# Three pairs without slot sums where score tiles change tokens, slots without a row spread over the rest, row buffers lent later once

## The chip, the cores and the metric

The kernel runs on one core of a Trainium2 chip. The metric is the device time of one execution in microseconds (us); the median of several executions counts. TensorE is called PE in the profile (its weight loads PEld), VectorE is DVE, ScalarE is ACT, GpSimd is POOL, and SyncE (SP) issues most transfers.

## The reference

The input is 2048 tokens of width 512. A layer norm `xn` feeds two branches, and the result is `x + A(xn) + B(xn)`.

```python
# A: attention, 32 heads of width 16 that share one k and one v
q = (xn @ wq).reshape(B, S, H, Dh).transpose(0, 2, 1, 3)
scores = jnp.einsum("bhqd,bkd->bhqk", q, xn @ wk) * (Dh ** -0.5)
A = heads_joined(softmax(scores) @ (xn @ wv)) @ wo
# B: product-key experts, H = 32, E = 64 keys on each side, K = 2
q = jnp.einsum("nd,dhc->nhc", xf, w_q)          # 2 halves of 128
s1, s2 = q1 @ k1.T, q2 @ k2.T                   # 64 scores each
i1, i2 = top 2 of each;  cand = the 4 sums;  top_e = the best 2 of 4 (rows of u and v)
g = softmax(top_s)
act = gelu(einsum("nd,nhkd->nhk", xf, u[top_e]))
out = einsum("nhk,nhk,nhkd->nd", g, act, v[top_e])
```

So each token takes 64 expert rows of 4096: a dot with `u`, a gelu and a gate, and a weighted sum of `v`.

## The kernel before

**Pairs.** After a start phase the kernel runs a list of 256 steps, `d` = 0 to 255. Each step is a *pair*: attention over two blocks of 128 keys for one unit (512 queries, 4 heads; 16 blocks make a unit, 32 units in all). `att_steps` emits for a pair, in this order: four score matmul groups (`sc`, L326) whose exponentials ScalarE writes to `pt` (L329), the `pv` matmuls of the pair before (L340), then `mid()`, four more score groups, perhaps an output projection (`block_out`, `pwo`), and `fill()`. All engines take their instructions in the order in which this list emits them.

**The expert branch** lies beside attention in the same pairs. Tokens are split into four groups of 512. For groups 0 and 1 the experts are *gathered*: 512 slots, each one row of `u` and `v` for 128 tokens. `gather` (L970, POOL) brings 128 rows of 4 KB into a row buffer `g`; `dot` (L982, DVE) multiplies with the token; ScalarE's tanh makes the gelu; `add` (L1017, DVE) adds the weighted `v` row to the token's total. This last is a *slot sum*. For groups 2 and 3 the experts are computed *densely* (`dense`: one-hot gates, then 32 blocks of `pact`, L727, and `pout`, L855). Before either, the scores of all four groups are computed by `item`: one item is 128 tokens by 8 score halves, 12 matmuls `psc` (L531) in four parts of three, then 8 MAX8 (L544) and 8 FIND_INDEX8 (L546) on VectorE. PSUM has three `x` buffers for this.

**Who sets the order.** `score_thread` is a generator of items and dense blocks; `fill()` advances it by parts until a planned amount (`aim`, at most `MOST`) is reached. The order of groups and weight chunks is `SEQ`: group 0 (8 chunks), group 1 (2 chunks), group 2 (8, then its dense part), group 1 (6 more), group 3 (8, then its dense part). Where the group changes, the four `xt` tiles (512 KB each) of the new tokens replace the old ones: `load_phase2_xt` (L1086, on SP's queue) issues each as soon as the last item of the old group has used its predecessor. SP also issues the reads of score weights (`wp_read`, L504: `wk<-dw`).

**The slots' pace.** `mid()` emits `todo` dots, a weight step, and `sums` slot sums; each slot sum sets one row buffer free, and `gathers(4)` then issues as many gathers as buffers are free, at most four:

```python
todo = max(min(int(pos + 0.001), g_next[0]) - d_next[0], 0)
sums = min(a_ready[0] - a_next[0], max(todo, 3) if d < half else 4)
if dense_on[0] > 2: sums = min(sums, 2)
if quiet[0] > 0: quiet[0] -= 1; sums = 0
while g_next[0] < NSL and g_next[0] < a_next[0] + NGB - lent[0] and most > 0: gather(...)
```

`pos` grows per pair by a rate that depends on the stage: 2.1 while group 0 is scored, 1.75 later (2.3 for 12 pairs after a dense part), 2.6 in a dense part, and in the last quarter what is left over what remains of the list. `g_next`, `d_next` and `a_next` count gathers, dots and sums; `a_ready` is the number of slots whose tanh has been issued (in fours). There are `NGB` = 12 row buffers; `lent` = 2 holds two of them back for the output weights `wo`, from the pair that sets it until the last of four `block_out`s. `quiet` exists already: in each dense part it stops the sums for three pairs at the end of the one-hot stage.

The gather of a token tile's first slot also loads that tile's `xa` (totals and normed tokens) through SP's queue.

Of the kernel before, what the change touches and what calls it, by code (L numbers as in the profile page):

```python
# [34 lines left out]
TPH = GT  # L35
NPH = NGRP
NSP = 2
NB = 32
# [17 lines left out]
def tile_kernel(ctx, tc, x, wq, wkv, wo, wqT, kT, uv, ub, vb, out):  # L56
# [416 lines left out]
    def wk_tile():  # L473
        return big.tile([P, 2, 512], F32R, name="wk", tag="wk", bufs=NWK)
# [26 lines left out]
    def wp_read(n, ks=range(KC)):  # L501
        for k in ks:
            wk = wk_tile()
            nc.sync.dma_start(raw(wk[:]), d_w[SEQ[n][1]][:, k])  # L504
            WC.setdefault(n, []).append(wk)
# [6 lines left out]
    def item(n_, ti, make=()):  # L512
        ph, c = SEQ[n_]
        nph, nc_ = SEQ[n_ + 1] if n_ + 1 < len(SEQ) else (None, None)
        t = TPH * ph + ti
        g, j = divmod(t, GT)
        b, jb = divmod(ti, BT)
        if jb == 0:
            m8 = small.tile([P, BT, 8, 8], F32, name="m8", bufs=1)
            i8 = small.tile([P, BT, 8, 8], U32, name="i8", bufs=1)  # L520
            M8[ph, c, b], I8[ph, c, b] = m8, i8
        m8, i8 = M8[ph, c, b], I8[ph, c, b]
        p = xtile("psc")

        last = ti == TPH - 1
        more = nc_ is not None and not (ph >= NSP and c == NC - 1)
        read = more and n_ + 1 >= NC
        n = 0
        for k in range(KC):
            for a, bb in TERMS:  # L530
                nc.tensor.matmul(p, XT[g][k][:, a, j * P:(j + 1) * P], WC[n_][k][:, bb, :],  # L531
                                 start=n == 0, stop=n == 11)
                n += 1
            if read and ti == 0 and k < 2:
                wp_read(n_ + 1, range(2 * k, 2 * k + 2))
            if last and more and nph != ph:
                load_phase2_xt(nph, k)
            if k < KC - 1:
                yield 3 * UNIT
            if k == 1:  # L540

                yield from islice(make, 1)
        for s in range(8):
            nc.vector.max(m8[:, jb, s, :], p[:, s * E:(s + 1) * E])  # L544
        for s in range(8):
            nc.vector.max_index(i8[:, jb, s, :], m8[:, jb, s, :], p[:, s * E:(s + 1) * E])  # L546
        if jb == BT - 1:
            batch(ph, c, b)
        yield 3 * UNIT
# [100 lines left out]
    def dense(DG, after):  # L650
# [211 lines left out]
        for b in range(NB):  # L862
            wd = []
            if b > 1:
                if b not in halved:

                    yield None
                if b not in halved:
                    flush()
                p = xtile("pact")  # L870
                for k in activations(b, splits[b][0], p):
                    if k == 0:
                        store(lambda b=b: fetch_gates(b + 1))
                        if b % 2 == 0 and b > 2:
                            later_split(b + 2)
                        if b == 2:

                            store(load_totals)
                    if k == KC - 1 and b == NB - 1 and after is not None:
                        wp_read(after, range(2))  # L880
                    if b == NB - 1 and after is not None:
                        load_phase2_xt(SEQ[after][0], k)
                    if k < KC - 1:
                        yield 3 * UNIT

                if b not in fetched:
                    if b > 3 and formed[0] < b - 2:
                        flush()
                    run(STORES)
                    assert b in fetched  # L890
            vs = splits.pop(b)[1]
            gy = gates[b]
            if b > 2:
                gates.pop(b - 1)
            g, y = (gy[:, 0, :], gy[:, 1, :]) if b > 1 else (gy[:, b, :], hh[:, b, :])

            def gated(g=g, p=None):
                stt(g, g, 1.0 / GS, p, op0=OP.mult, op1=OP.mult)

            def whole(y=y, g=g):  # L900
                stt(y, y, 1.0, g, op0=OP.add, op1=OP.mult)

            def scaled(y=y, g=g):
                multiplied[0] += 1
                stt(g, g, 1.0 / GS, y, op0=OP.mult, op1=OP.mult)

            def high(y=y if b > 1 else g, wd=wd):
                wd.append(late[0].tile([P, 2, 512], F32R, name="wd", tag="wd", bufs=4))
                nc.scalar.copy(wd[0][:, 0, :], y)
                behind(lambda: low(y, wd[0]))  # L910

            def low(y, wd):
                nc.vector.tensor_tensor(out=wd[:, 1, :], in0=y, in1=wd[:, 0, :], op=OP.subtract)  # L913
                formed[0] += 1

            if b > 1:
                nc.scalar.activation(y, p, AF.Square, scale=C_CUB ** 0.5)
                stt(y, y, C_IN, p, op0=OP.add, op1=OP.mult)
                LAST.append(lambda y=y: nc.scalar.activation(y, y, AF.Tanh))
                if b == 3:  # L920

                    behind(lambda gated=gated, g=g, p=p: gated(g, p))
                else:
                    gated(g, p)
                behind(whole)
                LATER_ACT.append(high)
            else:
                LATER.append(lambda scaled=scaled, high=high: (behind(scaled), on_act(high)))
            held.append((wd, vs))
            if b > 1:  # L930
                yield 3 * UNIT
            if b == 3:
                later_split(4)
            if b == 4:
                dense_on[0] = 1
            for _ in range(b - 1 if b in (2, 3) else 0):
                if out_ready():
                    block_out()
                    yield 3.6
            if b % 2:  # L940
                if b > 1:
                    later_split(b + 2)
                if ready:
                    for _ in range(2):
                        if formed[0] < used[0] + 2:
                            yield None
                    yield from sums()
                ready, held = held, []
# [73 lines left out]
    g_next, d_next, a_next, a_ready = [0], [0], [0], [0]  # L1022
# [90 lines left out]
    dense_on, quiet = [0], [0]  # L1113
# [19 lines left out]
    STEPS = 512  # L1133


    def att_steps(d, mid, fill):
        i = 2 * d
# [40 lines left out]
        if i == STEPS + 2:  # L1178
            last_out_a(3)
            last_out_b()  # L1180
        if i >= 124 and i % 128 == 124 or i == STEPS - 30:
            lent[0] = 2
        if 128 <= i < STEPS and i % 128 == (26 if i // 128 == 2 else 10) or i == STEPS - 10:
            load_wo()
# [57 lines left out]
    with tc.manual_schedule(engines={E_.PE, E_.Activation, E_.DVE, E_.Pool, E_.SP}):  # L1242
        done0 = spent[0]
        half = STEPS // 2
        pos, since = 0.0, half
        for d in range(half + 24):
# [6 lines left out]
            else:  # L1253
                pos += (2.1 if len(IDX) < NC * TPH else 2.3 if 0 <= d - since < 12 else 1.75, 0, 1.4, 1.5, 0.5)[dense_on[0]]

            todo = max(min(int(pos + 0.001), g_next[0]) - d_next[0], 0)

            def mid():
# [107 lines left out]
```

## Time and profile before

| what | value |
|---|---|
| median of 3 runs | 1934.66 us (1933.02 to 1942.46) |
| the profiled execution, its own time | 1943.82 us |
| its span, first to last instruction | 1942.1 us |
| mean granted PE clock | 0.978 |
| PE, DVE, ACT, POOL busy | 1870.5, 1675.0, 1294.5, 562.6 us |
| bytes moved by DMA | 491.11 MB, 253 GB/s over the span |

The start phase takes the first 138.6 us; then come the 256 pairs. A pair with 15 `psc`, `pact` or `pout` matmuls beside attention takes 6.81 us, one with 18 takes 7.49 us. A pair's start is taken as the start of its first exponential (every fourth `pt` row of L329). So pair 31 starts at 370.1 us, 34 at 389.3, 38 at 419.3, 41 at 443.3, 64 at 605.5, 65 at 618.9, 131 at 1065.6, 135 at 1093.2, 136 at 1102.9, 143 at 1151.2, 156 at 1241.3, 159 at 1260.4, 184 at 1442.0, 209 at 1597.1, 253 at 1905.1. Rows of a window give the time in which each engine was busy, the number of instructions in brackets, the granted clock and the share of the DMA engines.

### The profile page before, as it was taken

How to read it: one execution, taken by the hardware profiler on the slowest of the kernel's cores; microseconds unless marked ns; L12 is line 12 of the kernel's file. 1: busy time of each engine (PE TensorE's matmuls, PEld its weight loads, DVE VectorE, ACT ScalarE, POOL GpSimd, SP SyncE). 2: the span in 40 equal slices, each digit the busy share in tenths (PEclk: the TensorE clock that was granted, in tenths of full speed). 3: DMA queues.
4: the chain of work that ended last, by engine and by line, in shares of the span. 5: the costliest groups of instructions: out<-in, count | busy, mean ns of one | idle time of the engine just before them, and what ended most of it. 6: DMA issues, size and time to landing. Idle time of an engine off the chain costs nothing.

```text
span 1942.1 us, 34774 instructions
## 1 busy us (share of the span) xinstructions
PE 1870.5 (96%) x10990; PEld 994.7 (51%) x10990; DVE 1675.0 (86%) x6717; ACT 1294.5 (67%) x1803; POOL 562.6 (29%) x536
## 2 busy tenths in 40 slices
PE   6879999999999999999999999999999999999998
PEld 4634444555554544555555554555555445555553
DVE  6627788989999986899999897999999779999994
ACT  3236666655556887778778555655578877788873
POOL 1202223222221222344344423222212124344430
PEclk9979999999999889999999999999999899999999
DMA  7857879787773667798899988777746778989882
GB/s 272 316 178 257 276 269 305 278 299 239 235 254 106 197 223 244 247 287 286 276 281 299 375 284 262 256 236 260 235 126 223 240 227 279 286 265 297 279 276 84
DMA packets 234393, 491.11 MB, mean 253 GB/s; under 512 B 93396, under 2 KB 93396, under 8 KB 234204
## 3 DMA queue, kind: packets, MB, share of 16 engines
q0 software_dynamic: 73728, 268.47, 41.8%
q1 hardware_dynamic: 159240, 219.56, 34.9%
q8 instruction: 88, 1.44, 0.3%
q10 hardware_dynamic: 1236, 0.82, 0.1%
q14 instruction: 101, 0.83, 0.1%
HBM read 427.41 MB, written 56.07 MB: 249 GB/s over the span
## 4 chain that ended last, share of the span: by engine, by line
PE 70%; DVE 17%; ACT 2%; DMA 2%; issue 1%; SPq 0%; another core or an unknown queue 0%; ACTq 0%; DVEq 0%
PE pv L340 20%; PE sc L326 14%; PE psc L531 10%; PE pact L727 9%; PE pout L855 9%; DVE i L546 5%; PE pg L809 3%; DVE m L544 3%; DVE xa L1017 3%; PE pwo L433 2%; DVE g L982 2%; ACT pt L329 2%; PE pw L486 1%; DMA wqt<-in_wqT_dram 1%; DMA wk<-dw 1%
## 5 line engine op out<-in xcount | busy, mean ns | idle before, releaser
L329 ACT ACTIVATE pt<-sc 128x1024 f32<-128x1024 f32 x1024 | 993.5, 1026 | 461.2 <-PE sc L326 413.4
L970 POOL DMA_INDIRECT g<-in_uv_dram,idx x512 | 554.7, 1083 | 1325.5 <-DVE xa L1017 670.7
L340 PE MATMUL pv<-pt,vaug 128*32 128x512 f32 x4096 | 513.1, 619 | 0.0
L531 PE MATMUL psc<-wk,xt 128*128 128x512 f32 x1536 | 390.7, 402 | 9.5 <-DVE wk L496 2.9
L326 PE MATMUL sc<-qa,kaug 64*128 64x512 f32 x2048 | 386.7, 453 | 9.6 <-ACT pt L329 8.8
L1017 DVE SCALAR_TENSOR_TENSOR xa<-g,w,xa 128x512 f32<-128x512 f32 x512 | 372.5, 746 | 0.1
L982 DVE CUSTOM_DVE_ANT_0 g<-g,xa 128x512 f32<-128x512 f32 x512 | 335.5, 682 | 6.6 <-DMA g<-in_uv_dram,idx 6.6
L531 PEld LDWEIGHTS psc<-wk,xt 128*128 128x128 f32 x1536 | 278.2, 188 | 114.5 <-issue 38.0
L326 PEld LDWEIGHTS sc<-qa,kaug 64*128 64x128 f32 x2048 | 157.0, 186 | 331.5 <-ACT pt L329 205.7
L340 PEld LDWEIGHTS pv<-pt,vaug 128*32 128x32 f32 x4096 | 109.3, 111 | 256.4 <-issue 254.8
L546 DVE FIND_INDEX8 i<-m,psc 128x8 uint32<-128x64 f32 x1024 | 206.6, 222 | 0.0
L727 PE MATMUL pact<-xt,wk 128*128 128x512 f32 x768 | 197.6, 402 | 1.5 <-DVE i L546 1.1
L855 PE MATMUL pout<-wk,wd 128*128 128x512 f32 x768 | 194.9, 402 | 0.2 <-DVE wd L913 0.2
L544 DVE MAX8 m<-psc 128x8 f32<-128x64 f32 x1024 | 146.3, 215 | 27.6 <-PE psc L531 26.1
L727 PEld LDWEIGHTS pact<-xt,wk 128*128 128x128 f32 x768 | 140.0, 189 | 51.1 <-issue 17.9
L855 PEld LDWEIGHTS pout<-wk,wd 128*128 128x128 f32 x768 | 140.8, 188 | 47.4 <-DVE act L982 4.7
L692 DVE TENSOR_TENSOR wk<-rw,wk 128x512 fp32r<-128x512 f32 x128 | 85.0, 684 | 8.0 <-ACT wk L691 8.0
L858 DVE TENSOR_TENSOR da<-da,pout 128x512 f32<-128x512 f32 x128 | 82.9, 681 | 10.1 <-PE pout L855 9.4
L777 DVE TENSOR_TENSOR oh<-oh 128x2048 f16<-128x2048 f16 x64 | 78.0, 1219 | 2.2 <-PE pg L809 2.2
L809 PEld LDWEIGHTS <-oh 128*128 128x128 f16 x1024 | 68.4, 163 | 13.1 <-issue 4.6
L809 PE MATMUL pg<-oh 128*128 128x32 f16 x1024 | 73.6, 247 | 0.4 <-DVE oh L780 0.4
L691 ACT CAST wk<-rw 128x512 fp32r<-128x512 f32 x128 | 74.0, 631 | 0.0
(156 smaller groups left out, 1286.6 us busy)
## 6 DMA issues: line engine op xcount, KB each, us to landing
wk<-dw SPq DMA_DIRECT2D x96, 512.0 KB
wqt<-in_wqT_dram SPq DMA_DIRECT2D x32, 512.0 KB
dw<-wk SPq DMA_DIRECT2D x32, 512.0 KB
rw<-in_ub_dram SPq DMA_DIRECT2D x64, 256.0 KB
rw<-in_vb_dram SPq DMA_DIRECT2D x64, 256.0 KB
gy<-dg SPq DMA_DIRECT2D x64, 256.0 KB
qa<-dqh SPq DMA_DIRECT2D x128, 64.0 KB
g<-in_uv_dram,idx POOLq DMA_INDIRECT x512
```

The costliest lines, as they stand in the source:

```text
L326: nc.tensor.matmul(p[:, b, :], kaug[o:o + 64, kc * P:(kc + 1) * P], QA[u][o:o + 64, i, :], start=True, stop=True)
L329: nc.scalar.activation(pt, p, AF.Exp, scale=SCALE)
L340: nc.tensor.matmul(PV[u][32 * j:32 * j + 32, :], vaug[:, kc, :], pt[:, b, :], start=kc == 0, stop=kc == 15)
L531: nc.tensor.matmul(p, XT[g][k][:, a, j * P:(j + 1) * P], WC[n_][k][:, bb, :], start=n == 0, stop=n == 11)
L544: nc.vector.max(m8[:, jb, s, :], p[:, s * E:(s + 1) * E])
L546: nc.vector.max_index(i8[:, jb, s, :], m8[:, jb, s, :], p[:, s * E:(s + 1) * E])
L727: nc.tensor.matmul(p, us[:, a, k * P:(k + 1) * P], XT[DG][k][:, c, :], start=n == 0, stop=n == 11)
L809: nc.tensor.matmul(p[:, i * NB:(i + 1) * NB], oa[:, :, i], ob[:, :, i], start=True, stop=True)
L855: nc.tensor.matmul(p, wd[0][:, a, j * P:(j + 1) * P], vs[:, c, :], start=n == 0, stop=n == 5)
L970: nc.gpsimd.indirect_dma_start(out=gt, out_offset=None, in_=uv, in_offset=bass.IndirectOffsetOnAxis(ap=IDX[ph, c, ti][:, s:s + 1], axis=0))
L982: nc.vector.tensor_tensor_reduce(u, u, XN[TPH * ph + ti], scale=1.0, scalar=0.0, op0=OP.mult, op1=OP.add, accum_out=a[:, i:i + 1])
L1017: nc.vector.scalar_tensor_tensor(acc, v, w[:, i:i + 1], acc, op0=OP.mult, op1=OP.add)
```

## The change

```diff
@@ item(n_, ti, make), before the psc matmuls
         read = more and n_ + 1 >= NC
+        if ti == TPH - 2 and more and nph != ph:
+            quiet[0] = 3
@@ dense(DG, after), parts of block b
                     if k == KC - 1 and b == NB - 1 and after is not None:
                         wp_read(after, range(2))
+                    if k == 0 and b == NB - 1 and after is not None:
+                        quiet[0] = 3
@@ att_steps, end
-        if i >= 124 and i % 128 == 124 or i == STEPS - 30:
+        if i >= 124 and i % 128 == 124 and i // 128 != 1 or i == 272 or i == STEPS - 30:
             lent[0] = 2
@@ the loop over pairs, after pos has grown
+            pos = min(pos, g_next[0] + 1.0)
             todo = max(min(int(pos + 0.001), g_next[0]) - d_next[0], 0)
```

Four places set `quiet`: the last item but one of a group that is followed by another group (three times), and the first part of the last dense block of group 2. For the next three pairs `mid()` then emits no slot sum, so no row buffer comes free and no gather is issued either. `lent` = 2 is set at the end of pair 136 instead of pair 126 (`i` = 2`d`; `wo` is loaded in pair 141 as before). `pos` may run ahead of the gathers by one slot at most; what it loses there is made up where its rate is "what is left over what remains".

## The prediction

> **What bounds the kernel now.** The page comes first: who is busy, and what a slot costs VectorE.
>
> ```profile
> span 1942.1 us, 34774 instructions
> PE 1870.5 (96%) x10990; PEld 994.7 (51%) x10990; DVE 1675.0 (86%) x6717; ACT 1294.5 (67%) x1803; POOL 562.6 (29%) x536
> PE 70%; DVE 17%; ACT 2%; DMA 2%; issue 1%; SPq 0%; another core or an unknown queue 0%; ACTq 0%; DVEq 0%
> L1017 DVE SCALAR_TENSOR_TENSOR xa<-g,w,xa 128x512 f32<-128x512 f32 x512 | 372.5, 746 | 0.1
> L982 DVE CUSTOM_DVE_ANT_0 g<-g,xa 128x512 f32<-128x512 f32 x512 | 335.5, 682 | 6.6 <-DMA g<-in_uv_dram,idx 6.6
> ```
>
> PE is busy 96% of the span, and the chain of waits runs through it for 70% and through VectorE for 17%. A slot sum costs 372.5/512 = 0.73 us of VectorE, a dot 335.5/512 = 0.66 us. A mean says nothing of a stage, so the windows view comes next, with its edges at pair starts: pairs 31-33, 34-37, 38-40, 41-63 and 64.
>
> ```profile
> core 0: us, PE busy (x) PEld busy (x) DVE busy (x) ACT busy (x) POOL busy (x), PEclk, DMA share, GB/s
> 370.10:389.30 19.20, 17.82 (x107) 9.15 (x105) 18.89 (x117) 12.37 (x16) 6.32 (x7) 1.00 0.86 311
> 389.30:419.30 30.00, 30.00 (x170) 17.25 (x168) 27.54 (x193) 15.77 (x19) 5.75 (x6) 1.00 0.79 271
> 419.30:443.30 24.00, 21.67 (x116) 11.57 (x114) 18.89 (x109) 12.39 (x17) 6.45 (x7) 0.93 0.79 286
> 443.30:605.50 162.20, 161.51 (x917) 89.50 (x915) 158.79 (x1062) 93.86 (x115) 38.21 (x38) 1.00 0.70 228
> 605.50:618.90 13.40, 9.48 (x47) 5.10 (x45) 10.78 (x48) 7.15 (x11) 4.76 (x4) 0.78 0.50 133
> ```
>
> This is the view that decides. In the 162.2 us of pairs 41-63 VectorE is busy 158.8 us, 98%: it has 0.15 us free per pair. When the dense part begins (pair 64), PE stands idle for 13.40 - 9.48 = 3.9 us. I read this as VectorE falling behind through the stage and PE waiting at its end. So both engines bound this stage, and what VectorE can't do before it is paid in it. The same windows for pairs 131-134, 135, 136-142, 156-158, 159-183 and 209-252:
>
> ```profile
> 1065.60:1093.20 27.60, 27.60 (x158) 14.94 (x156) 23.45 (x59) 18.18 (x24) 10.80 (x10) 1.00 1.04 365
> 1093.20:1102.90 9.70, 7.89 (x44) 4.24 (x42) 7.66 (x39) 3.98 (x6) 4.22 (x5) 1.00 1.03 391
> 1102.90:1151.20 48.30, 48.30 (x278) 26.82 (x276) 46.98 (x285) 28.23 (x35) 13.34 (x13) 1.00 0.91 321
> 1241.30:1260.40 19.10, 18.63 (x110) 9.64 (x108) 15.73 (x103) 11.60 (x13) 4.02 (x4) 1.00 0.71 245
> 1260.40:1442.00 181.60, 177.15 (x1020) 98.84 (x1018) 176.18 (x1143) 105.29 (x133) 43.01 (x42) 1.00 0.67 223
> 1597.10:1905.10 308.00, 307.27 (x1732) 168.18 (x1730) 292.65 (x690) 241.12 (x344) 124.19 (x110) 1.00 0.87 275
> ```
>
> Now the four changes of tokens. Where PE waits there, the timeline of PE shows it; first the change from group 1 to group 2 (pair 39):
>
> ```profile
> 411.82 1.92 PE L340 MATMUL pv<-pt,vaug 128*32 128x512 f32 x16
> 419.31 1.92 PE L340 MATMUL pv<-pt,vaug 128*32 128x512 f32 x16
> 424.19 1.92 PE L340 MATMUL pv<-pt,vaug 128*32 128x512 f32 x16
> 431.38 3.53 PE L531 MATMUL psc<-wk,xt 128*128 128x512 f32 x9 [2.33 <-DMA xt<-dxt]
> 435.85 1.92 PE L340 MATMUL pv<-pt,vaug 128*32 128x512 f32 x16
> ```
>
> From `pv` to `pv` a pair with 18 `psc` takes 419.31 - 411.82 = 7.49 us; pair 39, which also has 18, takes 435.85 - 424.19 = 11.66. So 4.2 us are lost to the wait for `xt`, with what hangs on it (9 matmuls in 3.53 us are at a lower clock: 0.93 in that window). The change from the dense part back to group 1 (pair 135):
>
> ```profile
> 1093.29 1.92 PE L340 MATMUL pv<-pt,vaug 128*32 128x512 f32 x16
> 1096.42 0.97 PE L531 MATMUL psc<-wk,xt 128*128 128x512 f32 x3 [0.54 <-DMA wk<-dw]
> 1098.66 3.70 PE L531 MATMUL psc<-wk,xt 128*128 128x512 f32 x15 [1.27 <-DMA wk<-dw]
> 1102.95 1.93 PE L340 MATMUL pv<-pt,vaug 128*32 128x512 f32 x16
> ```
>
> Again 18 `psc`: 9.66 instead of 7.49 us, 2.2 lost. At the other two changes, pairs 31-33 and 156-158, PE is idle only 1.4 and 0.5 us, and no wait for a transfer is behind it. Whatever the change frees, these two stalls, 4.2 + 2.2 = 6.4 us, are what can be gained.
>
> **What the change does to the stalls.** The chain of waits names both transfers, and the timelines of SP and POOL show what moves beside them:
>
> ```profile
> 423.51 7.83 DMA xt<-dxt
> 1073.91 11.02 DMA dinv<-rc
> 1086.25 12.36 DMA wk<-dw
> ```
>
> ```profile
> 422.81 1.02 SPq L1086 DMA_DIRECT2D xt<-dxt  x2
> ```
>
> ```profile
> 423.02 1.20 POOL L970 DMA_INDIRECT g<-in_uv_dram,idx  x1 [13.24 <-DVE xa L1017]
> 425.78 0.94 POOL L970 DMA_INDIRECT g<-in_uv_dram,idx  x1 [0.30 <-DVE i L546]
> 1069.34 1.21 POOL L970 DMA_INDIRECT g<-in_uv_dram,idx  x1 [4.31 <-DVE gq L991]
> 1084.34 0.94 POOL L970 DMA_INDIRECT g<-in_uv_dram,idx  x1 [0.31 <-issue]
> ```
>
> At 422.81 SP issues the last two `xt`, 1.0 MB. Three gathers of 0.5 MB each start between 423.02 and 425.78, and `xt` lands at 431.3. With `quiet` set in pair 37 the sums of pairs 38-40 go, and with them these gathers: at the 365 GB/s of a window whose DMA share is 1.04, 1.0 MB takes 2.9 us, so even with 2 us ahead of it it is there at 427.7, before PE reaches it at about 429 (nine `psc` from 426.7). I take the whole 4.2 us off. At pair 135 the eight gathers from 1069.34 to 1084.34 (3 + 3 + 2, the sums of pairs 131-133) go: 4.2 MB, 11 us of that traffic. `dinv`, on which SP waits 11 us before it can issue the `wk` reads, lands earlier, and so do they. I take 2.2 us off. Bounds: nothing, and all 6.4.
>
> **What is put back.** I counted the slots through the rules of the loop, pair by pair, before and after. Sums per pair:
>
> | pairs | before | after |
> |---|---|---|
> | 31-33 | 3 1 3 | 0 0 0 |
> | 34-37 | 1 3 1 0 | 3 3 3 3 |
> | 38-40 | 3 1 3 | 0 0 0 |
> | 41-46 | 1 3 1 3 1 0 | 3 3 3 3 3 1 |
> | 131-135 | 3 3 2 3 3 | 0 0 0 3 3 |
> | 136-142 | 2 3 1 3 3 2 3 | 3 3 3 3 3 3 3 |
> | 156-158 | 0 3 1 | 0 0 0 |
> | 159-165 | 3 1 3 1 0 3 1 | 3 3 3 3 3 1 0 |
>
> Dots fall away in pairs 133 (3 to 1) and 134 (2 to 0), where the cap on `pos` holds; from there to the last quarter the slots run about four behind, and pairs 209-252 make them up. Nothing else caps it before the end. No sum is saved; each is moved into a later pair, so the question is VectorE's free time there.
>
> *Groups 0 to 2.* VectorE's idle time in pairs 31-40 is 0.31 + 2.46 + 5.11 = 7.9 us. After: pairs 31-33 lose 7 sums, 7 x 0.73 = 5.1 us, and PE's time there stays, so 5.4 idle. Pairs 34-37 get the 5.1 back; all but some 0.6 of their 2.46 is filled and VectorE enters pair 38 about 3.2 late. Pairs 38-40 lose 7 sums again and the stall: 5.11 - 4.2 + 5.1 - 3.2 = 2.8 idle. In sum 5.4 + 0.6 + 2.8 = 8.8, which is 0.9 more than before. The 5.1 us of pairs 41-46 then fall into the stage that has 0.15 us free per pair. So PE comes 4.2 us earlier into that stage, and VectorE, with the same work and 0.9 us more idle time behind it, leaves it 0.9 us later: **+0.9** (-4.2 if VectorE's lateness doesn't reach PE, +2 if less of the 5.1 fits into pairs 34-37).
>
> *Back to group 1.* Stall -2.2. Four sums, 2.9 us, go into pairs 136-142, where VectorE has 48.30 - 46.98 = 1.3 us free; pairs 144-150 have only one item in two pairs, so it recovers there. And dots now follow their gathers by about one pair (pairs 135-138): I add 1.0 for both (0 to 5). Sum **-1.2**.
>
> *To group 3.* No stall to win. Four sums, 2.9 us, move from pairs 156-158 (where VectorE idles 19.10 - 15.73 = 3.4 already) into the stage of pairs 159-183, 97% busy on VectorE, with PE idle 181.60 - 177.15 = 4.4 us towards its end. About 0.4 is hidden: **+2.5** (0 to 2.9).
>
> *Last quarter.* Four slots of 0.73 + 0.66 us are 5.5 us more for VectorE in pairs 209-252, which has 308.00 - 292.65 = 15.3 us free while PE has none: hidden but for **+0.5** (0 to 3). The buffers lent ten pairs later cost nothing: the sums that go in pairs 131-133 would leave no row at all otherwise.
>
> Sum: 0.9 - 1.2 + 2.5 + 0.5 = **+2.7 us**. The profiled execution took 1943.82 us by its own time, 9.2 above the median of 1934.66, so it becomes 1946.5; on the median that is **1937.4 us**, +0.14%. About 0.5%, 9.7 us, is what a measurement of this kernel can tell from no change, so this is none.
>
> **Rivals.** *VectorE's lateness is hidden.* The three PSUM buffers of the scores let VectorE be an item or two late. If that is room enough for 5 us, both stalls are pure gain and the rest nothing: 1934.66 - 6.4 = 1928.3. Against it speaks PE's idle time at the ends of both stages.
>
> *Dots wait for rows (slower).* After the quiet pairs the gathers are just ahead of the dots. How long a row takes under load, the timelines of POOL and DVE show for slot 416:
>
> ```profile
> 1638.83 2.24 POOL L970 DMA_INDIRECT g<-in_uv_dram,idx  x1 [0.30 <-issue]
> 1647.08 0.71 DVE L982 CUSTOM_DVE_ANT_0 g<-g,xa 128x512 f32<-128x512 f32 x1 [1.12 <-DMA g<-in_uv_dram,idx]
> ```
>
> 8.2 us from gather to dot, of which VectorE waited 1.1. Decisive is whether a row takes longer than a pair, 6.8 us. At pair 135 the transfers are at share 1.03; moreover the new tokens' `xa` are asked for two pairs later, behind six `wk` reads in SP's queue. If rows take the 12.4 us that `wk<-dw` took there, each of pairs 135-138 waits 12.4 - 6.8 = 5.6 us, 22.4 in all; less the 3.3 us that VectorE has free in pairs 135-142 and some 6 us that PE runs on with its score buffers, 13. With that for the 1.0 above: 1937.4 - 1.0 + 13 = 1949. The Trainium skill's page "TensorE: Matmul & The Clock Gate" (section on the array of 16 sub-arrays) says that VectorE's queue is strictly first in, first out; by that rule the waiting dot holds all MAX8 behind it, and the kernel comes to these 1949 us. Slot 416's row agrees that VectorE stood. Against the rival: the eight gathers' traffic is gone just then.
>
> *The `xt` stall stays.* Pair 37 now issues three gathers where it issued none, just ahead of the `xt` loads. If these hold `xt` up as the others did, 4.2 us aren't won: 1937.4 + 4.2 = 1941.6. Against it: POOL's row shows 13.2 us without a gather before 423.02, so the queue is empty then. The same page's section on HAM oscillation says that PE falls to half clock after about 3.4 us of idleness; by that rule a stall merely shortened would also run its nine matmuls at full clock, and this rival would cost less than 4.2. The clock row, 0.93, agrees that it fell; the idle time shown, 2.33 us, is less than the rule asks for.
>
> **How the numbers follow.** VectorE takes it back (1937.4): 0.50. Hidden (1928.3): 0.22. Dots wait (1949): 0.15. `xt` stall stays (1941.6): 0.13. Faster by over 0.5% (below 1925.0) needs the second case with more than I see in it: 0.07. Slower (above 1944.3): three quarters of the third, a quarter of the fourth, a little of the first: 0.17. The rest, 0.76, is the same. The range goes from 1927, just under the second case, to 1948, short of the third.
>
> **What would show it.** Right: no PE wait for `xt<-dxt` or `wk<-dw` at the two changes, pairs 39 and 135 at 7.5 us; no gathers for three pairs there; VectorE idle some 5 us more in pairs 31-33; later MAX8 in pairs 44-63, and more PE idle time in pair 64 and in pairs 176-184. Wrong: VectorE waiting for `g` for more than some us around pair 136 (third case), or a stage of pairs 41-64 shorter in step with PE (second).

## The result, and the profile after

The changed kernel takes **1960.53 us** (median of 4 runs, 1958.52 to 1964.63) against 1935.64 us for the kernel before on the same chip (4 runs, 1933.02 to 1942.46): a ratio of 1.0125, 95% interval 1.0094 to 1.0157. That is 24.9 us slower, and outside the range of the prediction. The profiled execution took 1960.91 us by its own time, 0.4 above its median.

The page of the changed kernel, with the lines that answer to those of before (line numbers are up to four higher):

```profile
span 1959.2 us, 34772 instructions
PE 1878.6 (96%) x10990; PEld 997.3 (51%) x10990; DVE 1675.7 (86%) x6717; ACT 1294.4 (66%) x1803; POOL 563.2 (29%) x536
PE 63%; DVE 23%; issue 3%; DMA 2%; ACT 2%; POOL 0%; SPq 0%; ACTq 0%; DVEq 0%; POOLq 0%
L1021 DVE SCALAR_TENSOR_TENSOR xa<-g,w,xa 128x512 f32<-128x512 f32 x512 | 372.8, 745 | 0.2
L986 DVE CUSTOM_DVE_ANT_0 g<-g,xa 128x512 f32<-128x512 f32 x512 | 335.4, 681 | 24.7 <-DMA g<-in_uv_dram,idx 24.7
```

VectorE does the same work (1675.7 us against 1675.0), but in the chain of waits its share rose from 17% to 23%, and the dots now wait 24.7 us for gathered rows instead of 6.6. This one line already points at the place where the prediction put 1.0 us. The windows of the changed kernel at the pairs used before: 31-33, 34-37, 38-40, 41-63, 135, 136-142, 143-146, 159-183 and 209-252.

```profile
368.80:389.70 20.90, 19.51 (x107) 9.34 (x105) 15.11 (x114) 12.34 (x17) 0.00 (x0) 0.92 0.76 260
389.70:419.60 29.90, 29.90 (x170) 17.27 (x168) 29.51 (x181) 15.68 (x18) 10.85 (x11) 1.00 0.69 239
419.60:444.60 25.00, 21.54 (x116) 11.54 (x114) 17.84 (x132) 12.45 (x17) 1.69 (x2) 0.93 0.71 247
444.60:615.10 170.50, 163.99 (x917) 89.65 (x915) 161.87 (x1053) 93.93 (x115) 44.63 (x44) 0.99 0.69 230
1096.70:1104.20 7.50, 7.50 (x44) 4.32 (x42) 1.79 (x5) 3.90 (x5) 0.00 (x0) 1.00 0.97 350
1104.20:1160.20 56.00, 51.66 (x278) 27.37 (x276) 50.88 (x303) 28.35 (x36) 19.76 (x19) 0.94 0.83 282
1160.20:1191.40 31.20, 29.43 (x144) 12.70 (x144) 30.76 (x173) 16.26 (x20) 11.05 (x11) 0.95 0.83 283
1272.60:1457.80 185.20, 179.84 (x1020) 100.19 (x1018) 179.04 (x1144) 105.26 (x133) 49.71 (x48) 0.98 0.69 226
1613.50:1922.30 308.80, 307.52 (x1732) 168.44 (x1730) 297.30 (x705) 241.26 (x345) 128.25 (x114) 1.00 0.89 280
```

The one stage that was not shown of before, its pairs 143-146, and the dense part's first pairs 65-85 (here matmuls are short and the clock changes from run to run), before:

```profile
1151.20:1178.50 27.30, 27.30 (x144) 12.40 (x142) 26.99 (x153) 16.35 (x21) 9.58 (x11) 1.00 0.85 259
618.90:751.00 132.10, 130.62 (x1058) 65.14 (x1056) 109.36 (x227) 107.11 (x173) 24.64 (x22) 0.89 0.63 207
```

and pairs 65-85 after:

```profile
628.50:754.70 126.20, 125.04 (x1058) 64.30 (x1056) 109.65 (x227) 106.99 (x173) 24.98 (x22) 0.93 0.67 216
```

Stage by stage, after minus before: pairs 31-33 +1.7, 34-37 -0.1, 38-40 +1.0, 41-63 +8.3, pair 135 -2.2, 136-142 +7.7, 143-146 +3.9, 159-183 +3.6, 209-252 +0.8. These stages sum to 24.7 us, near the 24.9 of the medians, but they are a choice, and one pair of traces. The two spans differ by only 17.1 us, since the profiled run of before was 8.2 us above its median of 4 runs. Pairs 65-85, which no edit touches, account for 5.9 us, at a clock of 0.89 against 0.93; in the traces of this case they take 125.5 to 135.6 us. And the 1.7 us of pairs 31-33 can't be put down to the change: three kernels that edit nothing there (the first, fourth and sixth experiment) take 20.8 to 20.9 us, too. In all five traces PE waits 1.4 us at the turn from pair 32 to 33; behind that wait the kernel before ran on at full clock, and the other four ran at half clock for a window of 3.4 us.

**The stall for `xt` (pair 39) stayed.** From the chain of waits, then POOL's and PE's timelines of the changed kernel:

```profile
423.17 8.98 DMA xt<-dxt
```

```profile
417.76 0.94 POOL L974 DMA_INDIRECT g<-in_uv_dram,idx  x1 [4.80 <-DVE den L608]
419.07 1.28 POOL L974 DMA_INDIRECT g<-in_uv_dram,idx  x1 [0.38 <-DVE gy L996]
420.66 0.93 POOL L974 DMA_INDIRECT g<-in_uv_dram,idx  x1 [0.30 <-DVE m L546]
432.19 4.35 PE L533 MATMUL psc<-wk,xt 128*128 128x512 f32 x12 [3.46 <-DMA xt<-dxt]
```

The gathers that used to start at 423.02 are gone, and three others stand in their place: those of pair 37, which makes up the sums of pairs 31-33. They start 2.5 to 5.4 us ahead of the last `xt` loads, whose tile lands after 8.98 us instead of 7.83. PE waits 3.46 us instead of 2.33.

**Dots wait for rows, and PE for the dots.** Timelines of POOL, DVE and PE around pairs 41-46:

```profile
448.95 1.27 POOL L974 DMA_INDIRECT g<-in_uv_dram,idx  x1 [27.36 <-DVE gq L995]
459.21 0.69 DVE L986 CUSTOM_DVE_ANT_0 g<-g,xa 128x512 f32<-128x512 f32 x1 [3.25 <-DMA g<-in_uv_dram,idx]
461.92 0.69 DVE L986 CUSTOM_DVE_ANT_0 g<-g,xa 128x512 f32<-128x512 f32 x1 [2.01 <-DMA g<-in_uv_dram,idx]
467.39 1.65 PE L533 MATMUL psc<-wk,xt 128*128 128x512 f32 x6 [2.26 <-DVE i L548]
491.47 0.98 PE L533 MATMUL psc<-wk,xt 128*128 128x512 f32 x3 [2.69 <-DVE i L548]
```

For 27.36 us POOL had nothing to gather, because no sum set a buffer free. The first gather after the pause starts at 448.95, its dot 10.3 us later, and VectorE stands for 3.25 us of them. Behind this dot in VectorE's queue are the MAX8 and FIND_INDEX8 that set the score buffers free; PE waits for them 2.26 us in pair 43 and 2.69 us in pair 46. The second of these waits is not the rows' alone: the sixth experiment below, which adds VectorE load and makes no row late, shows 1.58 us of it in the same pair.

In pairs 138 and 139 the same happens, and it reaches PE by another way, too. POOL, DVE, ACT and PE:

```profile
1114.43 1.35 POOL L974 DMA_INDIRECT g<-in_uv_dram,idx  x1 [5.22 <-DVE w L1009]
1123.33 0.69 DVE L986 CUSTOM_DVE_ANT_0 g<-g,xa 128x512 f32<-128x512 f32 x1 [4.31 <-DMA g<-in_uv_dram,idx]
1134.02 0.20 ACT L1002 ACTIVATE gth<-gy 128x4 f32<-128x4 f32 x1 [7.48 <-DVE gy L996]
1135.29 1.71 PE L326 MATMUL sc<-qa,kaug 64*128 64x512 f32 x4 [3.47 <-ACT pt L329]
1136.93 3.64 PE L340 MATMUL pv<-pt,vaug 128*32 128x512 f32 x16
```

From the start of the gather to its dot 8.9 us pass. The tanh of this group of four slots waits 7.48 us on ScalarE for its last dots, the exponentials of the attention stand behind it, and PE waits 3.47 us for them. What follows runs at half clock: 16 `pv` in 3.64 us instead of 1.92.

### The profile page after: what moved, and what is told of

The parts are those of the page before. It is cut to its first block, busy times and chain, and to the rows that moved or that the text cites. A ratio compares the mean times of both kernels' runs of the same rounds, so it can differ in the third digit from the quotient of the medians.

```text
span 1959.2 us, 34772 instructions
## 1 busy us (share of the span) xinstructions
PE 1878.6 (96%) x10990; PEld 997.3 (51%) x10990; DVE 1675.7 (86%) x6717; ACT 1294.4 (66%) x1803; POOL 563.2 (29%) x536
## 4 chain that ended last, share of the span: by engine, by line
PE 63%; DVE 23%; issue 3%; DMA 2%; ACT 2%; POOL 0%; SPq 0%; ACTq 0%; DVEq 0%; POOLq 0%
PE pv L340 18%; PE sc L326 12%; PE pact L729 9%; PE pout L857 9%; PE psc L533 8%; DVE i L548 6%; DVE xa L1021 4%; DVE m L546 4%; DVE g L986 3%; PE pg L811 3%; PE pwo L433 2%; DMA g<-in_uv_dram,idx 2%; PE pw L486 2%; ACT pt L329 1%; DVE oh L779 1%
## 5 line engine op out<-in xcount | busy, mean ns | idle before, releaser
L340 PE MATMUL pv<-pt,vaug 128*32 128x512 f32 x4096 | 518.9, 625 | 0.0
L986 DVE CUSTOM_DVE_ANT_0 g<-g,xa 128x512 f32<-128x512 f32 x512 | 335.4, 681 | 24.7 <-DMA g<-in_uv_dram,idx 24.7
```

Of the source, the lines that this page charges most:

```text
L340: nc.tensor.matmul(PV[u][32 * j:32 * j + 32, :], vaug[:, kc, :], pt[:, b, :], start=kc == 0, stop=kc == 15)
L986: nc.vector.tensor_tensor_reduce(u, u, XN[TPH * ph + ti], scale=1.0, scalar=0.0, op0=OP.mult, op1=OP.add, accum_out=a[:, i:i + 1])
```

## The experiments

Three theories were to be told apart: *rows* (the pause empties the stock of gathered rows, and the dots' waits at the head of VectorE's queue make the loss), *moved sums* (the sums that are made up fill VectorE), and, for the stall in pair 39, *gathers beside `xt`*. All comparisons had five rounds with the kernel before on the same chip; its medians there were 1936.48, 1938.87 and 1939.00 us. In the edits `n_` is the place in `SEQ`: 7 is the last chunk of group 0, 9 that of group 1 before group 2.

**One pause alone, from group 1 to group 2.** Before, plus:

```diff
+        if ti == TPH - 2 and more and nph != ph and n_ == 9:
+            quiet[0] = 3
```

> The kernel before with the three pairs without sums at one place only, the change from group 1 to group 2 (pairs 38-40; nothing in pairs 31-33, 131-133, 156-158, no cap on the position, the buffers lent as before). Theory 'rows' (the pause empties the stock of gathered rows, dots wait for them at the head of VectorE's queue and MAX8 behind them comes late): pairs 42-47 lose about what they lost in the changed kernel, 2.5 + 3.0 + 1.7 = 7.2 us. Theory 'three gathers ahead of xt' for the stall in pair 39: pair 37 now issues no gathers, so pair 39 comes down from 11.7 to about 7.5 us, 4.2 us won; together 1935.6 + 7.2 - 4.2 = 1938.6 us. If the xt stall has nothing to do with gathers, it stays and the time is about 1943. If the losses of pairs 42-47 came from the first pause (pairs 31-33) and not from this one: about 1931.4.

1945.61 us (median), ratio 1.0047 (1.0025 to 1.0069). PE's timeline of this run:

```profile
428.39 4.38 PE L533 MATMUL psc<-wk,xt 128*128 128x512 f32 x18
463.28 2.68 PE L533 MATMUL psc<-wk,xt 128*128 128x512 f32 x6 [1.93 <-DVE i L548]
```

The 18 matmuls of pair 39 run without a wait, so 4.1 us are won there, as expected where pair 37 gathers nothing. Pairs 43 to 56 lose 3.5 + 1.5 + 0.6 + 1.6 + 0.7 = 7.9 us, where 7.2 were expected. The net 3.8 us are less than the 9.1 that the ratio gives. Part of that, 1.6 us in pair 33 ahead of the pause, is clock, and the profiled execution, at 1940.55 us, was one of the shortest of the twelve; the rest I can't place.

**One pause alone, from the dense part back to group 1.** The changed kernel without its two lines in `item`.

> The changed kernel with its pause only at the change from the dense part back to group 1 (pairs 131-133); the cap and the buffers lent later are kept, nothing in pairs 31-33, 38-40, 156-158. Theory 'rows': 2.2 us won in pair 135 (no wait for wk), about 11.7 us lost in pairs 139-144 as in the changed kernel, so 1935.6 + 9.5 = about 1945 us, with VectorE waiting for g by about 10 us in pairs 135-138. Rival 'VectorE's load' (the sums made up in pairs 134-142 make MAX8 late, whatever the rows do): also slower, but by no more than the 2.9 us of the four sums, so about 1936. If the loss of the changed kernel is one of the whole program's clock and not of this place: 1933 to 1936.

1952.91 us, ratio 1.0066 (1.0038 to 1.0094), or 12.8 us. In its trace pair 135 has no wait of PE (-2.2), pairs 139, 140, 143 and 144 lose 5.5 + 2.7 + 2.6 + 1.7 = 12.5 us, and the dots wait 22.9 us for rows in all. The moved sums can't do this: they are 2.9 us.

**Gathers held back in program order, no pause of the sums.**

```diff
-            quiet[0] = 3   (both places)
+            hold[0] = 3
-                    gathers(4)
+                    if hold[0] > 0:
+                        hold[0] -= 1
+                    else:
+                        gathers(4)
```

> The changed kernel with one difference: in the three pairs after each change of tokens the slot sums are emitted as in the kernel before, and only the gathers are held back (for the same three pairs; afterwards up to four per pair). VectorE's sums so stay where they were, while the stock of rows ahead of the dots falls as in the changed kernel (2 rows in pairs 34 and 41, 1 and 0 in pairs 133 and 134). Theory 'rows': the loss stays although no sum is moved: 1950 to 1962 us, with VectorE's wait for g at about 20 us or more in all. Rival 'VectorE's load': with no sum moved there is no loss, and the xt and wk stalls may shrink: 1930 to 1937 us.

1938.63 us, ratio 1.0010 (0.9987 to 1.0032): no loss, which looks like the end of the theory of rows. The timelines of POOL and DVE say otherwise:

```profile
420.73 1.20 POOL L974 DMA_INDIRECT g<-in_uv_dram,idx  x1 [13.25 <-DVE xa L1021]
450.41 0.69 DVE L986 CUSTOM_DVE_ANT_0 g<-g,xa 128x512 f32<-128x512 f32 x1
```

This is slot 84, whose gather was emitted in pair 41. POOL executed it at 420.73, in pair 38, right when the sum had set its buffer free: POOL's queue was empty, so a later place in the program was no later time. The rows were 30 us ahead. The experiment didn't delay what it was to delay.

It tells two other things. The rules for `todo` and the cap count gathers by their place in the program, so from pair 133 on the dots fall away as in the changed kernel: 87 dots and 83 sums stand later among VectorE's instructions than before. Yet pairs 136-142 take what they take before, so this order costs nothing as long as the rows are early:

```profile
1090.70:1139.00 48.30, 48.30 (x278) 26.82 (x276) 45.57 (x283) 28.23 (x35) 11.27 (x11) 1.00 0.86 293
```

And the stall of pair 135 is gone:

```profile
1085.78 4.37 PE L533 MATMUL psc<-wk,xt 128*128 128x512 f32 x18
```

The eight gathers of pairs 131-133 ran here as in the kernel before, and SP waited for `dinv` as long as before (11.0 us, from 1064.10 to 1075.06). So it is not shown that taking these gathers away is what ends that stall. One thing did move here as in the changed kernel: SP issues the reads of the new tokens' `xa` behind the six `wk` reads and not ahead of them. That alone doesn't end it either: in the tenth experiment `xa` comes behind them, too, and pair 135 takes 9.7 us.

**No pause at all: the cap and the later lending alone.** The changed kernel without its four `quiet` lines.

> The changed kernel without any of the new pauses: only the cap on the position and the row buffers lent ten pairs later once. By both theories the cap never binds and two rows more are ahead in pairs 128-136, which nobody waits for: same time as before, 1935.6 us within 0.3%; VectorE's wait for g not above the 6.6 us of before. If lending later matters by itself: more than 5 us off.

1936.91 us, ratio 0.9993 (0.9974 to 1.0012): no cost of these two edits shows, as expected.

**Rows really late, no pause of the sums.** The changed kernel, `hold[0] = 9` in place of `quiet[0] = 3`, and POOL made to wait for VectorE:

```diff
-                    gathers(4)
+                    if 0 < hold[0] <= 6:   # one column of the pair's last sum (or dot)
+                        nc.gpsimd.tensor_copy(late_s, ...)
+                    if hold[0] <= 6:
+                        gathers(3 if hold[0] else 4)
+                    hold[0] = max(hold[0] - 1, 0)
```

> The changed kernel with the slot sums emitted as in the kernel before, but with the gathers issued in the same pairs as in the changed kernel: none for three pairs, then three per pair, and this time really late, because POOL reads (one column, ahead of the gathers) a result that VectorE writes in that same pair. In the run that held the gathers back by program order alone they were not late: slot 84 was gathered at 420.7 us, 30 us ahead of its dot, as soon as its buffer came free. Theory 'rows alone' (late rows are enough for the loss, no sum need be moved): VectorE waits for g by about 20 us in all, pairs 42-47 and 139-144 lose 5 to 12 us each as in the changed kernel, 1946 to 1960 us. Theory 'both' (VectorE's waits cost only where the sums made up leave it no slack): waits for g appear, but much of them is covered: 1938 to 1946 us. Theory 'moved sums alone': 1934 to 1938 us, and no PE wait for FIND_INDEX8 in pairs 43-47 or 139-143.

1961.60 us (4 runs), ratio 1.0127 (1.0109 to 1.0145): the whole loss. Up to pair 132 dots and sums are emitted as in the kernel before; from there on they stand later, exactly as in the third experiment, where they cost nothing. The two kernels give VectorE the same dots and sums in the same order, and differ in when the rows come: after the pause at the dense part, dots 268 to 279 start 4.9 to 13.5 us after their gathers here, and 21.7 to 33.5 us there. Its group of dots, and its windows of pairs 41-63 and 136-142:

```profile
L986 DVE CUSTOM_DVE_ANT_0 g<-g,xa 128x512 f32<-128x512 f32 x512 | 335.2, 680 | 35.7 <-DMA g<-in_uv_dram,idx 35.7
```

```profile
447.60:616.10 168.50, 163.61 (x917) 89.93 (x915) 159.11 (x1061) 94.17 (x115) 44.73 (x50) 0.99 0.70 233
1104.80:1163.60 58.80, 51.06 (x276) 26.97 (x274) 47.24 (x300) 27.99 (x36) 19.26 (x24) 0.97 0.80 279
```

That is 6.3 and 10.5 us more than before. One reservation: POOL waits here for the last sum of a pair, so in pair 41 the gathers start 6.7 us after the pair's start, against 4.3 us in the changed kernel, and the dots wait 35.7 us instead of 24.7. That late rows are enough is shown; the exact share in the changed kernel is not.

**Load alone.** The kernel before, with

```diff
                     gathers(4)
+                    for _ in range({41: 2, 43: 2, 45: 2, 46: 1, 136: 1, 138: 2, 141: 1}.get(d, 0)):
+                        ...
+                        nc.vector.scalar_tensor_tensor(acc, acc, 0.0, acc, op0=OP.mult, op1=OP.add)
```

> The kernel before with eleven more VectorE instructions of the size of a slot sum (0.73 us each; they add zero times the total to the total), at the places and in the number of the sums that the changed kernel makes up: 2, 2, 2, 1 in pairs 41, 43, 45, 46 and 1, 2, 1 in pairs 136, 138, 141. The gathers stay as they are. Theory 'rows' for the second place: VectorE has 3.3 us free there, so four instructions of 2.9 us cost nearly nothing in pairs 136-144; at the first place VectorE is 98% busy and the seven cost at most their own 5.1 us: 1936.5 + 5 = about 1941 us. Theory 'moved sums alone': the extra load does what the changed kernel's sums did, some 7 us lost in pairs 41-47 and 10 in pairs 136-144: about 1953 us.

1941.12 us, ratio 1.0023 (1.0010 to 1.0036), 4.5 us. The same two windows:

```profile
441.10:607.90 166.80, 162.42 (x917) 89.32 (x915) 163.25 (x1068) 94.00 (x115) 38.54 (x38) 1.00 0.66 221
1107.30:1155.60 48.30, 48.30 (x278) 26.81 (x276) 47.75 (x287) 28.22 (x36) 12.56 (x13) 1.00 0.92 326
```

Seven instructions of 5.1 us cost 4.6 us in pairs 41-63, and four of them nothing in pairs 136-142. The way in which the prediction priced VectorE's load holds; the moved sums alone don't make the loss. In pairs 41-63 they make a good part of it, though: the changed kernel loses 8.3 us there, the load alone costs 4.6, and the late rows alone (the fifth experiment, where they are later than in the changed kernel) 6.3. So the two overlap, and their shares there are not parted; in pairs 136-142 it is the rows.

**Pauses of one pair.** The changed kernel with `quiet[0] = 1` at both lines.

> The changed kernel with pauses of one pair instead of three at all four places (the cap and the later lending kept). The stock of rows then falls to 5 and 3 at the least and is back after two pairs; pair 37 issues no gathers, so none stand ahead of xt. Theory 'rows' with 'three gathers ahead of xt': no wait of the dots for g beyond the 6.6 us of before, pair 39 at about 7.5 us (4.2 won), the wk stall of pair 135 smaller: 1929 to 1934 us. Theory 'moved sums alone': three moved sums per place cost 2.2 us each in the full stages: 1936 to 1941 us.

1942.27 us, ratio 1.0026 (1.0011 to 1.0042). Pair 39 takes 8.8 us, 3.0 less than in the trace of before; but it takes 8.6 and 9.0 us in the second and sixth experiments, too, where nothing is edited at that place, so no gain is shown. The dots wait 11.5 us, not 6.6, and PE shows where:

```profile
1081.00 5.91 PE L857 MATMUL pout<-wk,wd 128*128 128x512 f32 x13 [4.19 <-DVE wd L917]
```

At the end of the dense part the stock is only three or four rows, one pair's pause is enough for a wait, and there PE hangs on `wd`, which VectorE makes behind the dots. Pair 133 takes 14.8 us instead of 7.8. My expectation had counted the rows, and not that two or three of them are used per pair there.

**The gathers of pair 38 behind `xt`.** The kernel before; `hold[0] = 2` in `item` where `n_ == 9`, and

```diff
+                    if hold[0] == 1:
+                        nc.gpsimd.tensor_copy(late_s, XT[2][3][:, 0, :1])
+                    if hold[0] < 2:
                         gathers(4)
+                    hold[0] = max(hold[0] - 1, 0)
```

> The kernel before with one edit, at the change from group 1 to group 2 alone: no sum is moved; the three gathers of pair 38 are issued only after the last xt tile has landed (POOL reads one column of it first). Theory 'gathers beside xt make the stall of pair 39': pair 39 falls from 11.7 to about 7.6 us and nothing is lost later, since seven rows stand ahead of the dots: 1936.5 - 4 = about 1932.5 us. If xt is late by itself: unchanged, 1936.5 us.

1938.97 us, ratio 1.0014 (0.9997 to 1.0031). POOL and PE:

```profile
430.56 0.19 POOL L1304 COPY late_s<-xt 128x1 f32<-128x1 f32 x1 [18.73 <-DMA xt<-dxt]
428.75 4.38 PE L533 MATMUL psc<-wk,xt 128*128 128x512 f32 x18
```

PE no longer waits for `xt`, and pair 39 takes 7.6 us: it is the gathers that make this stall. Pairs 41-63 take 162.2 us as before. Yet the 4.1 us don't show in the whole: the interval begins at 0.9997 and leaves room for a gain of 0.6 us at most. Part of the answer is that the trace of before has a long stall. In the four other kernels that edit nothing there (experiments two, four, six and eleven) pair 39 takes 8.6, 11.6, 9.0 and 11.4 us; with before that is 10.5 on average, so some 2.9 us are to be won, not 4.1. In this profile pair 135 is also 1.6 us longer. Where the rest went is open.

**The first pause alone.** As in the first experiment, with `n_ == 7` (pairs 31-33).

> The kernel before with the three pairs without sums only at the change from group 0 to group 1 (pairs 31-33). The stock falls to 2 rows here too, but the rows for the first dots after it were gathered with 6.6 us to spare in the changed kernel and no dot waited. Theory 'rows', with VectorE's idle time as the price: pairs 31-33 idle 5.4 us more, some 2 us of it taken back in pairs 34-37, so up to 3.5 us lost in pairs 46-56; pair 37 issues three gathers, so the xt stall stays (pair 39 at 11.7 to 12.8 us). About 1936.5 + 4 = 1940.5 us. If the catch-up gathers of pair 37 don't hold up xt: pair 39 at 7.6 us and about 1936 us.

1946.20 us, ratio 1.0033 (1.0012 to 1.0054). PE in pair 39, and the window of pairs 41-63:

```profile
434.76 1.65 PE L533 MATMUL psc<-wk,xt 128*128 128x512 f32 x3 [4.70 <-DMA xt<-dxt]
```

```profile
450.30:612.60 162.30, 161.58 (x917) 89.59 (x915) 158.89 (x1062) 93.89 (x116) 38.19 (x38) 1.00 0.69 227
```

With the gathers of pair 37 and those of pair 38 both around the loads, pair 39 takes 16.8 us, 5.0 more than before. Pairs 41-63 lose nothing, where I had expected up to 3.5 us; that VectorE catches up during the longer stall is my reading, and no run tests it. This pause costs by what its catch-up does to `xt`. The 1.6 us that pairs 31-33 take more stand in kernels without an edit there, too.

**Dots stopped with the sums (group 1 to group 2).** The first experiment, plus

```diff
-            quiet[0] = 3
+            quiet[0], stop[0] = 3, 3
...
+            if stop[0] > 0:
+                stop[0] -= 1       # pos stands still
+            elif dense_on[0] == 1:
-            if dense_on[0] == 1:
```

> As the kernel with the pause only at the change from group 1 to group 2 (pairs 38-40), which lost 9.1 us by its median, with one thing more: the dots stop for the same three pairs, and the position with them, so no row is used and seven stay in stock; the five or six slots that fall away are made up in the last quarter. Theory 'rows': no dot waits for g in pairs 42-43 any more, and pairs 42-47 take what they take in the kernel before (43 at 7.5, 46 at 6.8 us); pair 39 at 7.6 us as before with no gathers beside xt: 1936.5 - 4 = 1932 to 1937 us, the upper end if the last quarter shows the later slots. Rival 'any pause of VectorE's slot work costs': VectorE idles still longer in pairs 38-40 (8.5 us of work fall away), so the loss is as large or larger: 1943 to 1948 us.

1939.98 us, ratio 1.0008 (0.9985 to 1.0032). Pairs 38-40 and 41-63:

```profile
422.30:442.20 19.90, 19.90 (x116) 10.77 (x114) 12.80 (x103) 12.34 (x16) 0.00 (x0) 1.00 0.66 230
442.20:605.20 163.00, 161.18 (x917) 89.64 (x915) 159.47 (x1056) 93.86 (x114) 40.25 (x40) 1.00 0.68 228
```

VectorE idles 7.1 us in pairs 38-40, as much as in the changed kernel (25.00 - 17.84 = 7.2), and yet pairs 41-63 take 163.0 us and not 170.5. So the idle time of the pause isn't the harm. Here no rows are missing afterwards and no sums are made up in pairs 41-46 either, so this run doesn't part these two; the fifth and sixth do. The whole is no shorter than before, where 1932 to 1937 us were expected, although pair 39 takes 7.7 us.

**The same at the dense part.** The second experiment without the cap, with `quiet[0], stop[0] = 3, 3`.

> As the kernel with the pause only at the change from the dense part back to group 1 (pairs 131-133), which lost 12.8 us by the ratio, but without the cap and with the dots and the position stopped in the same three pairs: six rows stay in stock; eight slots are made up in the last quarter. Theory 'rows': no wait for g of more than some us in pairs 134-138, pairs 139, 140, 143, 144 back at 6.8 us, pair 135 at 7.5 us (2.2 us won); the eight slots are 11 us more for VectorE in a last quarter where it has 15 us free, 0 to 4 us: 1934 to 1939 us. Rival 'any pause costs': about 1953 us again.

1945.90 us, ratio 1.0036 (1.0014 to 1.0059). Pairs 135, 136-142 and 209-252:

```profile
1088.80:1096.30 7.50, 7.50 (x44) 4.31 (x42) 6.04 (x36) 3.99 (x6) 3.92 (x4) 1.00 1.01 384
1096.30:1144.60 48.30, 48.30 (x278) 26.82 (x276) 47.09 (x286) 28.23 (x35) 13.65 (x13) 1.00 0.89 316
1593.70:1906.30 312.60, 308.88 (x1732) 169.22 (x1730) 301.50 (x721) 241.49 (x345) 151.53 (x118) 0.99 0.89 284
```

The stall of pair 135 is gone and pairs 136-142 take what they took before: with six rows in stock the 10 us vanish. But the eight slots that are put off come back: pairs 209-252 take 4.6 us more and pairs 159-183 1.9, where 0 to 4 were expected, and the whole stays slower than before. Of the 4.6 us, 3.8 are lost in pair 213:

```profile
1626.04 4.61 PE L855 MATMUL pout<-wk,wd 128*128 128x512 f32 x12 [2.21 <-DVE gy L900]
```

VectorE makes this `gy` behind a dot that has just stood 4.93 us for its row. So here, too, it is late rows more than VectorE's load.

**Both cures together**, the run just told plus the gathers of pair 38 behind `xt`.

> A version meant to beat both: the pause of sums and dots at pairs 131-133 as in the run before in this list, and at the change from group 1 to group 2 no pause, but the three gathers of pair 38 issued only once the last xt tile has landed (this took pair 39 from 11.8 to 7.6 us). Theory 'rows': 4.1 us won in pair 39 and 2.2 us in pair 135, less 0 to 4 us in the last quarter: 1930 to 1935 us. If a microsecond won at a stall is given back elsewhere: 1936 to 1940 us.

1945.46 us, ratio 1.0030 (1.0012 to 1.0047). Pair 39 at 7.7 us and pair 135 at 7.5 are both as meant; pairs 209-252 take 5.2 us more, and pairs 159-183 2.0, so the time lies above both ranges of the expectation. No version here beats the kernel before. In these last two, the slots put off give back what is won at the stalls; in the eighth nothing is put off, and the gain doesn't show all the same.

## Why the prediction was wrong, point by point

Two steps failed. "I take the whole 4.2 us off" left out what the gathers of pair 37 do to `xt`. And dots that wait for late rows were booked with 1.0 us at one place and with nothing at the other; some 11.6 us came of it behind the dense part, and in pairs 41-63 some 3.2 us beyond the load that was booked.

**The bounds** were read from one trace: 4.2 + 2.2 = 6.4 us. In kernels that edit nothing at these places pair 39 takes 8.6 to 11.8 us and pair 135 7.9 to 11.3, against 7.5 without a stall. So the stalls are 1.1 to 4.3 and 0.4 to 3.8 us long, and the one of pair 39 was booked near its upper end.

**The stall at pair 135: right in size, cause not shown.** Pair 135 takes 7.50 us, and 2.2 us are won against the trace of before. But the prediction won them by taking the eight gathers away and so having `dinv` land earlier, and in the third experiment the stall goes with all eight in place and `dinv` as late as before. What ends it is open.

**The stall at pair 39: wrong.** "I take the whole 4.2 us off" was the step; pair 39 takes 12.8 us, 1.0 more than in the trace of before. The rival "the `xt` stall stays" named the reason, the three gathers of pair 37, and I set it aside because POOL's queue was empty for 13.2 us before 423.02. That row was of before: in the changed kernel pair 37's own gathers fill just this gap. Without gathers in pair 37 (the first experiment) or with pair 38's behind the loads (the eighth) the 4.1 us do appear.

**Groups 0 to 2, +0.9: wrong, +10.9 measured** (1.7 - 0.1 + 1.0 + 8.3). The counting of VectorE's idle time was good where it dealt with work: 5.4 us foretold for pairs 31-33 and 20.90 - 15.11 = 5.8 measured (in part luck: VectorE's busy time fell by 3.8 us, not by the 5.1 of the sums, and 1.7 us came from the slower clock); 0.6 and 0.4 for pairs 34-37; and the extra load alone cost 4.6 for 5.1. For pairs 38-40 it gave 2.8 us, and 7.2 came, since the stall stayed. What the sum had no term for are the dots' waits in pairs 42-43, 5.3 us of VectorE's time. For pairs 41-63 the +0.9 implied 0.9 + 4.2 = 5.1 us more, and 8.3 came, so the waits added some 3.2 us to what the load would have cost. I had counted the slots and knew how far the gathers were ahead, but put a price on dots behind their gathers for pairs 135-138 only.

**Back to group 1, -1.2: wrong, +9.4 measured** (-2.2 + 7.7 + 3.9). The mis-sized term is "I add 1.0 for both (0 to 5)": 7.7 + 3.9 = 11.6 us came, and as the load alone cost nothing in pairs 136-142 and 0.2 us in pairs 143-146, they are the late rows'. This is the rival "dots wait for rows", which gave 13 us for this place and was given a chance of 0.15. Its decisive point, that a row takes longer than a pair of 6.8 us, was met: 8.9 us for the row that VectorE waited 4.31 us for. My argument against it, that the eight gathers' traffic is gone just then, fails on the window row of pair 135: the share of the DMA engines is still 0.97, with `wk` and `xa` reads and the three gathers issued just ahead of it. That VectorE's queue is first in, first out, as the Trainium skill's page "TensorE: Matmul & The Clock Gate" says in its section on the array of 16 sub-arrays, the trace bears out; the rule gave 1949 us, and the measured time is above that because the same wait came at pairs 42-43 as well and the stall of pair 39 stayed. The page says the same of ScalarE, and the tanh row (7.48 us, with the exponentials behind it) agrees.

**To group 3, +2.5: too high, as far as the traces part it.** Pairs 159-183 take 3.6 us more; but 2.0 of that stand in the second experiment, too, which has no pause at pairs 156-158 and whose slots run four behind. That leaves 1.6 for this pause. **Last quarter, +0.5: right**, +0.8. **The later lending at nothing: right** (ratio 0.9993).

**What would show it.** Three pairs without gathers and VectorE's idle time in pairs 31-33 are there; pair 135 takes 7.5 us, pair 39 doesn't. More idle time of PE in pair 64 isn't there (3.9 us before and after). The sign named for the third case, VectorE waiting for `g` around pair 136, is there with 10.9 us in pairs 135-138.

**The range** ended at 1948 because the two bad cases, each at one place, were taken one at a time. They have one cause, a pause in setting buffers free, which acts at every place where the pause stands; they should have been added up. Put right by what was measured, the sum of 2.7 grows by 10.6 (11.6 for 1.0 behind the dense part), 5.2 (+1.0 for -4.2 in pair 39), 3.2 (pairs 41-63), 1.7 (the clock in pairs 31-33) and 1.3 in the rest: 24.7, which is the sum of the stages above again and no second proof. The interval of the ratio stands for 18 to 30 us; its width is more than any of these terms.

## What to carry to other kernels

A step that sets buffers free also drives the prefetch: before you pause it, count how many items stand ahead of the consumer, and compare the pause with that stock and the time of one transfer under load; a consumer at the head of an in-order queue passes its wait to everything behind it. Moving a burst of transfers away from a critical load only helps if the burst that makes it up doesn't land on the next one. A stall is to be measured in several traces before it is booked as a gain: the one in pair 39 was 1.1 to 4.3 us long in kernels that were the same up to there. And a later place in the program delays nothing on an engine whose queue is empty: make it wait for a result, if it is to be late.

## What the runs showed of the hardware

PE's clock fell after shorter idleness than the rule cited in the prediction asks for. Windows of 3.4 us of the changed kernel, around PE's wait in pair 143:

```profile
1165.60:1169.00 3.40, 1.63 (x8) 0.80 (x8) 3.40 (x32) 0.00 (x0) 1.32 (x2) 1.00 0.97 339
1169.00:1172.40 3.40, 3.40 (x20) 0.72 (x18) 3.40 (x21) 1.94 (x2) 0.00 (x0) 0.50 1.01 395
```

PE is idle for 3.40 - 1.63 = 1.8 us, and the whole next window runs at 0.50. The Trainium skill's page "TensorE: Matmul & The Clock Gate" (section on HAM oscillation) speaks of some 3.4 us of idleness; here half of that was enough. Pair 144 so takes 1.5 us longer, pair 47 1.7 and pair 140 2.9, all without a wait of their own: with the pair ahead of it, the wait of 1.8 us in pair 143 cost 4.0 us.

Runs of one kernel spread by over 20 us (the kernel before took 1929.8 to 1954.1 us in one batch). In the profiled executions PE is at half clock for 14 to 38 us of pairs 65-85 alone, whatever was edited elsewhere. Two traces can differ by more than the 4 us that are at stake in one pair, so such a gain has to show in the medians, and in the eighth experiment it did not.
